# A linear-attention block with a routed MLP on one core: K's factor from one exponential, POOL's products moved, and the routing's work spread over six turns

## The chip, the core and the metric

The kernel runs on one core of a Trainium2 chip. Its time is the device time of one launch in microseconds; three runs of the kernel before took 224.96, 225.59 and 227.16 us, so the median is 225.59 us. A core has TensorE (PE, matrix products into PSUM), VectorE (DVE), ScalarE (ACT), GpSimd (POOL), and SyncE (SP), whose queue issues nearly all transfers here. Each engine takes its instructions in the order in which they were written, and waits at the first whose inputs or buffers are not ready.

## What is computed

Four batches of 768 tokens, 8 heads of 48 channels (C = 384). First a gated linear recurrence per head:

```python
for t in range(S):
    cur   = (u * k_t) outer v_t
    y_t   = r_t @ (state + cur)
    state = w_t[:, None] * state + k_t outer v_t
```

Then, on the heads laid side by side (x, 768 rows of 384 per batch), a routed MLP:

```python
scores  = x @ w_gate
top     = the 128 rows of the batch with the highest scores
out     = x
out[top] = x[top] + sigmoid(scores[top]) * (relu(x[top] @ w1) @ w2)   # w1 384x1024, w2 1024x384
```

## The kernel before

The recurrence is done in 24 chunks of 128 tokens (4 batches of 6), one chunk's output per turn of the loop at line 541; n numbers the turns, from -4 to 23. Decay products are taken in logs. For a chunk, `lnw` (L139, L143) takes lw = ln w and over = exp(-lw) on ACT. `sums` (L159) multiplies lw by a triangular matrix on PE, so that PSUM holds the log sums X; ACT then makes fall = exp(X) (L162), rise = exp(-X) (L165) and, from X's first row, the chunk's total decay in a line (L172), which a small transfer turns into a column, `all` (L176). `divided` (L183) makes kw = k * over on POOL, `scaled` (L216) K = kw * fall and R = r * rise on DVE. `turned` (L226, L228) transposes K and R on PE and copies them out on ACT. `scores` (L242), `fresh` (L258, the products of K and v, two halves per chunk), `masked` (L270, DVE), `states` (L285, L288 on DVE; L290 on POOL, mid * all), `from_state` (L301) and `from_chunk` (L318) make the chunk's output in the PSUM tile P, of which there are two. The token's own term goes beside: `own_products` (L192 r * k, L193 times u, both POOL), `own_sum` (L200, DVE), `own_values` (L207, POOL: vo = v * own). `result` (L332) adds P and vo into x on DVE, L338 takes the score, and L342 stores x.

The order is written out by hand. The loop body runs several chunks at once: turn n works on the state part of chunk n, the products of chunk n+1, the transposes of n+2, K and R of n+3 and the logs of n+4. The order within a turn is

```python
loads(n + 4); [one piece of w1 or w2, turns 2 to 8]
from_state(n); lnw(n + 4); divided(n + 3); scores(n + 1); fresh(n + 1); from_chunk(n)
mix(what[0]); turned(n + 2, "K"); turned(n + 2, "R"); masked(n + 1); states(n + 1); result(n)
sums(n + 4); scaled(n + 3); own_products(n + 3); own_values(n + 1); own_sum(n + 2); mix(what[1])
```

L192 carries an explicit wait (`sync`, L192): it starts only behind the same chunk's R on DVE. `loads(m)` (L107) issues on SP w of chunk m+4, k and r of m+3 and v of m+1, 192 KB each, from five or six buffers a name. SP's queue holds in a turn: four loads, a piece of a weight, the store of x, the `all` transfer. Ahead of the loop stand `loads(-4)` to `loads(-1)` and the broadcasts of u and w_gate (L508 to L513), 192 KB each too.

The routed part comes in two generators, taken in steps by `mix` from turn 6 on. `select(b)` (L349): copies every score to all partitions (L356 PE, L359 ACT), compares (L369, six DVE instructions), counts on PE (L379), ranks and picks on DVE (L384 to L393), turns the pick into indices (L400 PE, L404 DVE), gathers 128 rows with an indirect transfer on POOL's queue (L413), transposes them (L421, L423) and makes the gate (L428 to L444). `forward(b)` (L450): 8 steps of six products with w1 (L464), a relu on ACT every four steps (L469), 8 steps of products with w2 (L474), the gated sum on DVE (L480) and an indirect store (L483). A string such as "fssfsf" in `plan` (L493) says which steps, f or s, a turn takes. `forward(b)` begins in the fifth turn of the next batch. Behind the loop (L573) come a test of the value range, which all engines load (L581), the rest of `forward(2)`, `select(3)` and `forward(3)`.

PSUM's eight banks: four for the two P tiles, two shared by name "r" (transposes), one "m" (log sums, and select's products), one "f" (forward's products).

Of the kernel before, what the change touches and what calls it, by code (L numbers as in the profile page):

```python
# [35 lines left out]
def kernel(  # L36
# [30 lines left out]
    assert 0 < CAP < S and CAP % L != 1 and B * NCH < 256  # L67
# [26 lines left out]
    work = {n: {} for n in range(N)}  # L94

    def load(name, n):
        if not 0 <= n < N:
            return
        b, ci = chunks[n]
        x, bufs = dict(w=(w, 5), k=(k, 5), r=(r, 5), v=(v, 6))[name]  # L100
        t = lev.tile([L, H, D], FP32, tag=name, name=name, bufs=bufs)
        nc.sync.dma_start(  # L102
            out=t, in_=x[b, :, ci * L:(ci + 1) * L, :].rearrange("h t d -> t h d")
        )
        work[n][name] = t

    def loads(n):  # L107
        load("w", n + 4)
        load("k", n + 3)
        load("r", n + 3)  # L110
        load("v", n + 1)
# [23 lines left out]
    def lnw(n):  # L135
        if 0 <= n < N:
            t = work[n]
            t["lw"] = lev.tile([L, C], FP32, tag="lw", name="lw", bufs=2)
# [3 lines left out]
            t["over"] = lev.tile([L, C], FP32, tag="over", name="over", bufs=3)  # L142
            nc.scalar.activation(out=t["over"], in_=t["lw"], func=AF.Exp, scale=-1.0)  # L143
# [9 lines left out]
    def sums(n):  # L153
        if not 0 <= n < N:
            return
        t = work[n]
        lw = t.pop("lw")
        ps = psM.tile([L, 512], FP32, tag="m", name="ps_x")
        nc.tensor.matmul(ps[:, 0:C], tri, lw, start=True, stop=True)  # L159
        t["fall"] = lev.tile([L, C], FP32, tag="fall", name="fall")  # L160
        t["rise"] = lev.tile([L, C], FP32, tag="rise", name="rise")
        nc.scalar.activation(  # L162
            out=t["fall"], in_=ps[:, 0:C], func=AF.Exp, accum_out=guard[:, n, 1:2]
        )
# [4 lines left out]
        if chunks[n][1] > 0:  # L169
            line = line_bufs[n % len(line_bufs)]  # L170
            t["all"] = all_bufs[n % len(all_bufs)]
            nc.scalar.activation(  # L172
                out=line[:, :, 0:D, :].rearrange("o q d j -> o j q d"), func=AF.Exp,
                in_=ps[0:1, 0:C].rearrange("o (j q d) -> o j q d", q=2, d=D),
            )
            nc.sync.dma_start(out=t["all"], in_=line.rearrange("o q d j -> o (q d j)"))  # L176

    def divided(n):
        if not 0 <= n < N:
            return  # L180
        t = work[n]
        t["kw"] = lev.tile([L, H, D], FP32, tag="kw", name="kw")
        nc.gpsimd.tensor_mul(  # L183
            t["kw"], t["k"], t.pop("over").rearrange("p (h d) -> p h d", d=D)
        )

    def own_products(n):
# [4 lines left out]
        sync(nc.gpsimd.tensor_mul(rk, t.pop("r"), t.pop("k")), t["scaled"], "one port")  # L192
# [16 lines left out]
    def scaled(n):  # L209
# [5 lines left out]
        for to, of, by in (("K", "kw", "fall"), ("R", "r", "rise")):  # L215
            t["scaled"] = nc.vector.tensor_mul(  # L216
                t[to][:, :, 0:D], t[of], t.pop(by).rearrange("p (h d) -> p h d", d=D)
            )
# [126 lines left out]
    groups = [(c0, min(L, CAP - c0)) for c0 in range(0, CAP, L)]  # L345

    chosen = {}

    def select(b):  # L349

        every = mod.tile([L, S], FP32, name="every")
        for hf in range(2):
            ps = psM.tile([L, NHF, L], FP32, tag="m", name="ps_e")
# [9 lines left out]
            yield  # L363

        ahead = mod.tile([L, NCH, S], BF16, name="ahead")
        won = mod.tile([L, NCH], FP32, name="won", bufs=2)
        for c in range(NCH):
            lo = c * L
            nc.vector.scalar_tensor_tensor(  # L369
# [6 lines left out]
        ps = psM.tile([L, NCH], FP32, tag="m", name="ps_r")  # L376
        for c in range(NCH):
            for e in range(c + 1):
# [3 lines left out]
                )  # L382
        rank = mod.tile([L, NCH], FP32, name="rank", bufs=2)
        nc.vector.tensor_sub(rank, behind_n, won)  # L384
        nc.vector.tensor_add(rank, ps, rank)

        for gi, (c0, n) in enumerate(groups):
            pick = mod.tile([L, NCH, L], BF16, name="pick")
            at = rank
            if c0 > 0:  # L390
                at = mod.tile([L, NCH], FP32, name="at")
                nc.vector.tensor_scalar_add(out=at, in0=rank, scalar1=float(-c0))
            nc.vector.tensor_tensor(  # L393
                out=pick, in0=_heads(slots, NCH), in1=at.to_broadcast([L, NCH, L]),
                op=ALU.is_equal,
            )
            yield
            ps = psM.tile([L, 2], FP32, tag="m", name="ps_i")
            for c in range(NCH):
                nc.tensor.matmul(  # L400
                    ps, pick[:, c, :], ids[:, b, c, :], start=(c == 0), stop=(c == NCH - 1)
                )
            idx = mod.tile([L, 1], UINT32, name="idx", bufs=2)
            nc.vector.tensor_scalar(  # L404
                out=idx, in0=ps[:, 0:1], scalar1=ps[:, 1:2], scalar2=float(b * S),
                op0=ALU.add, op1=ALU.max,
            )
            rows = views[b][0:b + 1].rearrange("b s c -> (b s) c")
            where = bass.IndirectOffsetOnAxis(ap=idx[0:n, 0:1], axis=0)
            xe = mod.tile([L, C], FP32, name="xe", bufs=2)  # L410
            if n < L:
                nc.vector.memset(xe, 0.0)
            nc.gpsimd.indirect_dma_start(  # L413
                out=xe[0:n], out_offset=None, in_=rows, in_offset=where,
                bounds_check=(b + 1) * S - 1, oob_is_err=False,
            )
            yield

            ps = psM.tile([L, NDC, L], FP32, tag="m", name="ps_x")
            for dc in range(NDC):  # L420
                nc.tensor.transpose(ps[:, dc, :], xe[:, dc * L:(dc + 1) * L], ident)  # L421
            xeT = mod.tile([L, NDC, L], FP32, name="xeT", bufs=2)
            nc.scalar.copy(out=xeT, in_=ps)  # L423
            yield

            own = mod.tile([L, 1], FP32, name="own", bufs=2)
            scr = lev.tile([L, C], FP32, tag="scr", name="scr")
            nc.vector.tensor_tensor_reduce(  # L428
                out=scr, in0=xe, in1=wg_bc, scale=1.0, scalar=0.0, op0=ALU.mult, op1=ALU.add,
                accum_out=own,  # L430
            )
            neg = mod.tile([L, 1], FP32, name="neg", bufs=2)
            nc.vector.scalar_tensor_tensor(
                out=neg, in0=own, scalar=-1.0, in1=own, op0=ALU.mult, op1=ALU.min
            )
            nc.scalar.activation(out=neg, in_=neg, func=AF.Exp)
            den = mod.tile([L, 1], FP32, name="den", bufs=2)
            nc.vector.tensor_scalar_add(out=den, in0=neg, scalar1=1.0)
            nc.vector.reciprocal(out=den, in_=den)
            gate = mod.tile([L, 1], FP32, name="gate", bufs=2)  # L440
            nc.vector.scalar_tensor_tensor(
                out=gate, in0=own, scalar=0.0, in1=neg, op0=ALU.is_ge, op1=ALU.max
            )
            nc.vector.tensor_mul(gate, gate, den)  # L444
            chosen.setdefault(b, []).append((n, rows, where, xe, xeT, gate))
            yield
# [213 lines left out]
```

## Time and profile before

| | |
|---|---|
| median of three runs | 225.59 us |
| the profiled execution | 223.47 us, of it 221.6 us from the first to the last instruction |
| busy | PE 172.4, DVE 141.6, POOL 117.6, ACT 102.2 us |
| start of x (L332) in turns 0, 5, 11, 20, 23 | 27.87, 55.40, 100.35, 169.51, 188.67 us |
| transfers | 29.38 MB; four loads and one store of 192.0 KB a turn, 3 pieces of 512.0 KB and 4 of 384.0 KB |
| granted TensorE clock, mean | 0.931 |

How to read it: a page gives the busy time of each engine, the span in 40 slices, the chain of work that ended last, and the costliest groups of instructions with the idle time ahead of each and what ended it. The timeline gives every instruction's start and duration, so the starts of L332 mark the turns. Busy time is an average over stages; the prediction takes the stages one by one.

### The profile page before, as it was taken

To read this page: it belongs to the slowest core of one execution; us is meant where nothing else is said; L and a number is where in the kernel's file an instruction comes from. 1 tells how busy PE (TensorE), PEld (TensorE's weight loads), DVE (VectorE), ACT (ScalarE), POOL (GpSimd) and SP (SyncE) were. 2 spreads that over 40 slices of the span, in tenths; PEclk is the share of its full clock that TensorE was granted. 3 is DMA by queue.
4 is the path that set the end of the run, shared out by engine and by line. 5 is a ranking of instruction groups with operands and counts; after the bars stand their busy time and mean duration, and the time that the engine had idled before them with its cause. 6 is when DMAs were issued, how large, how long until landed. Compare 5 with 4: busy or idle time off the path is not lost.

```text
span 221.6 us, 8505 instructions
## 1 busy us (share of the span) xinstructions
PE 172.4 (78%) x3586; PEld 138.2 (62%) x3586; DVE 141.6 (64%) x329; ACT 102.2 (46%) x261; POOL 117.6 (53%) x137
## 2 busy tenths in 40 slices
PE   2697677797859766897799869978898598686990
PEld 0465466676648665796687657867876467553950
DVE  6443177777546998695769986976499834281301
ACT  4685645476852722755666426656642101110110
POOL 3750578887176669775546497745654931001101
PEclk9998899999985985999999969999999769999997
DMA  6998997878989996996899884622011022101101
GB/s 130 209 186 168 192 176 163 177 137 224 233 199 210 213 209 166 198 230 149 180 201 210 180 179 100 157 63 73 3 40 40 4 70 74 38 1 36 38 7 40
DMA packets 108542, 29.38 MB, mean 133 GB/s; under 512 B 103376, under 2 KB 107728, under 8 KB 108496
## 3 DMA queue, kind: packets, MB, share of 16 engines
q1 hardware_dynamic: 107984, 27.18, 56.5%
q0 software_dynamic: 512, 1.57, 2.1%
q8 instruction: 30, 0.49, 1.0%
q14 instruction: 16, 0.13, 0.2%
HBM read 23.20 MB, written 5.51 MB: 130 GB/s over the span
## 4 chain that ended last, share of the span: by engine, by line
PE 27%; DVE 21%; issue 13%; POOL 11%; DMA 9%; ACT 9%; SPq 8%; POOLq 0%; DVEq 0%; ACTq 0%
SPq L102 6%; DMA all_buf<-line_buf 5%; PE ps_p L318 5%; PE ps_f L464 5%; DVE ahead L369 5%; PE ps_t L226 5%; POOL rk L192 3%; DVE scr L338 3%; POOL vo L207 3%; DVE x L332 3%; PE ps_f L474 3%; POOL rk L193 2%; DVE k_buf L216 2%; DMA xe<-out_dram,idx 2%; PE ps_p L242 2%
## 5 line engine op out<-in xcount | busy, mean ns | idle before, releaser
L192 POOL TENSOR_TENSOR rk<-r,k 128x384 f32<-128x384 f32 x24 | 24.4, 1015 | 20.7 <-DVE r_buf L216 19.4
L228 ACT COPY Kt<-ps_t 128x512 f32<-128x512 f32 x24 | 14.0, 585 | 45.1 <-PE ps_t L226 45.1
L318 PE MATMUL ps_p<-v,sc 64*64 64x48 f32 x768 | 30.8, 230 | 4.4 <-issue 2.6
L290 POOL TENSOR_TENSOR s<-mid,all_buf 128x192 f32<-128x192 f32 x20 | 12.2, 610 | 38.7 <-DMA all_buf<-line_buf 24.1
L318 PEld LDWEIGHTS ps_p<-v,sc 64*64 64x64 f32 x768 | 28.0, 146 | 5.6 <-issue 3.0
L159 PE MATMUL ps_x<-lw,tri 128*128 128x384 f32 x48 | 23.9, 585 | 6.4 <-ACT lw L139 6.4
L369 DVE SCALAR_TENSOR_TENSOR ahead<-every,score,behind 128x768 bf16<-128x768 f32 (+5 forms) x24 | 23.4, 1024 | 8.2 <-ACT every L359 8.2
L464 PE MATMUL ps_f<-xeT,w 128*128 128x128 f32 x192 | 24.5, 278 | 4.5 <-ACT hid L469 3.9
L464 PEld LDWEIGHTS ps_f<-xeT,w 128*128 128x128 f32 x192 | 23.1, 192 | 7.5 <-ACT hid L469 4.5
L193 POOL TENSOR_TENSOR rk<-rk,u_bc 128x384 f32<-128x384 f32 x24 | 25.2, 1050 | 1.9
L183 POOL TENSOR_TENSOR kw<-k,over 128x384 f32<-128x384 f32 x24 | 24.4, 1018 | 3.0 <-DMA k<-in_k_dram 2.9
L474 PE MATMUL ps_f<-w,hid 128*128 128x384 f32 x64 | 25.3, 529 | 0.7 <-ACT hid L469 0.7
L270 DVE TENSOR_TENSOR sc<-ps_p,mask 128x512 f32<-128x512 f32 x24 | 16.4, 682 | 14.7 <-PE ps_p L258 14.7
L332 DVE TENSOR_TENSOR x<-ps_p,vo 128x384 f32<-128x384 f32 x24 | 13.3, 552 | 17.4 <-POOL vo L207 14.5
L207 POOL TENSOR_TENSOR vo<-v,own 128x384 f32<-128x384 f32 x24 | 23.2, 966 | 0.0
L242 PE MATMUL ps_p<-Rt,Kt 48*64 48x64 f32 x768 | 17.7, 229 | 5.6 <-DVE x L332 3.2
L301 PEld LDWEIGHTS ps_p<-s,Rt 48*64 48x64 f32 x704 | 13.5, 135 | 13.4 <-issue 7.3
L242 PEld LDWEIGHTS ps_p<-Rt,Kt 48*64 48x64 f32 x768 | 15.0, 141 | 7.3 <-ACT over L143 2.0
L226 PE MATMUL ps_t<-ident,k_buf 128*128 128x128 f32 x96 | 18.7, 327 | 0.0
L301 PE MATMUL ps_p<-s,Rt 48*64 48x48 f32 x704 | 16.4, 223 | 2.5 <-DVE mid L288 2.5
L474 PEld LDWEIGHTS ps_f<-w,hid 128*128 128x128 f32 x64 | 12.6, 208 | 8.0 <-issue 1.8
L226 PE MATMUL ps_t<-ident,r_buf 128*128 128x128 f32 x96 | 17.2, 310 | 0.0
(77 smaller groups left out, 301.8 us busy)
## 6 DMA issues: line engine op xcount, KB each, us to landing
w<-in_w_dram SPq DMA_DIRECT2D x24, 192.0 KB, 4.0
k<-in_k_dram SPq DMA_DIRECT2D x24, 192.0 KB, 4.4
r<-in_r_dram SPq DMA_DIRECT2D x24, 192.0 KB, 4.7
v<-in_v_dram SPq DMA_DIRECT2D x24, 192.0 KB, 4.0
out_dram<-x SPq DMA_DIRECT2D x24, 192.0 KB, 2.8
w<-in_moe_w_dram SPq DMA_DIRECT2D x3, 512.0 KB, 5.2
w<-in_moe_w_dram SPq DMA_DIRECT2D x4, 384.0 KB, 5.2
all_buf<-line_buf SPq DMA_DIRECT2D x20, 2.0 KB, 2.6
```

What stands on the lines that cost most here:

```text
L159: nc.tensor.matmul(ps[:, 0:C], tri, lw, start=True, stop=True)
L183: nc.gpsimd.tensor_mul(t["kw"], t["k"], t.pop("over").rearrange("p (h d) -> p h d", d=D))
L192: sync(nc.gpsimd.tensor_mul(rk, t.pop("r"), t.pop("k")), t["scaled"], "one port")
L193: nc.gpsimd.tensor_mul(rk, rk, u_bc)
L207: nc.gpsimd.tensor_mul(t["vo"], t["v"], t.pop("own").to_broadcast([L, H, D]))
L226: nc.tensor.transpose(ps[:, j, :], t[name][:, 2 * j:2 * j + 2, :], ident)
L242: nc.tensor.matmul(P[half(sub), par, j * HB:(j + 1) * HB], t["Kt"][half(par, D), j, half(sub)], t["Rt"][half(par, D), j, half(sub)], start ...
L301: nc.tensor.matmul(t["P"][half(sub), par, j * D:(j + 1) * D], t["Rt"][half(par, D), j, half(sub)], t["s1" if sub else "s0"][half(par, D), ...
L318: nc.tensor.matmul(t["P"][half(sub), par, j * D:(j + 1) * D], t["sc"][half(sub), par, j, :], t["v"][half(sub), 2 * j + par, :], start=(sub ...
L369: nc.vector.scalar_tensor_tensor(out=ahead[:, c, lo:S], in0=every[:, lo:S], scalar=score[:, b, c:c + 1], in1=behind[:, 0:S - lo], op0=ALU. ...
L464: nc.tensor.matmul(ps[:, q, :], w1[:, dc, (f0 + q) * L:(f0 + q + 1) * L], xeT[:, dc, :], start=(dc == 0), stop=(dc == NDC - 1),)
L474: nc.tensor.matmul(ps, hid[:, fc, :], w2[:, fc, :], start=(fc == 0), stop=(fc == NFC - 1))
```

## The change

- `over` and `kw` go. In their place `without` (DVE) takes X, read from PSUM, less the chunk's lw, and `falls` (ACT) makes fall = exp of that from SBUF; K = k * fall directly.
- `sums` keeps only the product and rise; fall and the total's line are made a turn later, the line by `totals`.
- POOL: L183 goes; vo is made at the head of the turn; r * k waits for the latest DVE instruction marked `latest["two"]`: R, or a comparison or pick that follows R in the turn. `own_sum` stays at the end of the turn, behind these.
- Loads: `loads(m)` comes at the end of a turn, behind the store of x, three chunks ahead instead of four, in the order v, k, r, w. `all` now stands in front of the store. k and r get six buffers, lw three. Ahead of the loop only `loads(-4)` to `loads(-2)` remain, and the first v (chunk 0) and v of chunk 1 are the 10th and the 14th of the 192 KB transfers on SP, where they were the 12th and the 17th.
- The routed part: `select` ends with the comparisons, `chosen_rows` (x) does ranks to transposes, `gates` (g) the gate. Their PSUM tiles move from bank "m" to the "r" pair and "f". A plan of six turns says what each does at three places; `forward(b)` begins six turns behind `select(b)` (turn 12 for batch 0) instead of four, so that `forward(2)` lies wholly behind the loop. There the order is written out in a string.

```diff
     def loads(n):
-        load("w", n + 4)
+        load("v", n + 1)
         load("k", n + 3)
         load("r", n + 3)
-        load("v", n + 1)
+        load("w", n + 4)
...
     def sums(n):
-        lw = t.pop("lw")
-        ps = psM.tile([L, 512], FP32, tag="m", name="ps_x")
-        nc.tensor.matmul(ps[:, 0:C], tri, lw, start=True, stop=True)
+        ps = t["X"] = psM.tile([L, 512], FP32, tag="m", name="ps_x")
+        nc.tensor.matmul(ps[:, 0:C], tri, t["lw"], start=True, stop=True)
...
+    def without(n):
+        t["less"] = lev.tile([L, C], FP32, tag="less", name="less")
+        nc.vector.tensor_sub(t["less"], t.pop("X")[:, 0:C], t.pop("lw"))
+
+    def falls(n):
+        t["fall"] = lev.tile([L, C], FP32, tag="fall", name="fall")
+        nc.scalar.activation(
+            out=t["fall"], in_=t.pop("less"), func=AF.Exp, accum_out=guard[:, n, 1:2]
+        )
...
-        sync(nc.gpsimd.tensor_mul(rk, t.pop("r"), t.pop("k")), t["scaled"], "one port")
+        sync(nc.gpsimd.tensor_mul(rk, t.pop("r"), t.pop("k")), latest["two"], "one port")
...
     plan = [
-        ("", "fsfsss"), ("", "fssfsf"), ("", "fsf"), ("s", "fff"), ("s", "sfff"), ("", "fff")
+        ("f", "sx", "ss"), ("", "ffff", "ss"), ("", "ff", "s"),
+        ("", "xff", "xx"), ("", "xffff", "xg"), ("g", "ffff", "g"),
     ]
...
+            from_state(n)
+            own_values(n + 1)
+            totals(n + 3)
+            without(n + 3)
+            lnw(n + 4)
+            scores(n + 1)
+            fresh(n + 1)
+            from_chunk(n)
+            turned(n + 2, "K")
+            turned(n + 2, "R")
+            falls(n + 3)
+            masked(n + 1)
+            states(n + 1)
+            result(n)
+            mix(what[0])
+            if n >= 2 * NCH and n % NCH == 0:
+                steps["f"] = forward(n // NCH - 2)
+            sums(n + 4)
+            mix(what[1])
+            scaled(n + 3)
+            mix(what[2])
+            own_products(n + 3)
+            own_sum(n + 2)
+            for m in range(max(n - 1, -4) if n <= AHEAD else n, n if n < AHEAD else n + 1):
+                loads(m + AHEAD)
...
+        mix("fsxffffsssssffffxxxffxx")
+        steps["g"] = gates(B - 2)
+        mix("gggffffff")
```

## The prediction

> **What bounds the kernel now.** I read the table of stages first, then the chain of waits inside one stage, then the timeline for the prices of single instructions. Stages, by the starts of x: up to turn 0, turns 0 to 5, 5 to 12, 12 to 18, 18 to 23, and what lies behind the loop.
>
> ```profile
> core 0: us, PE busy (x) PEld busy (x) DVE busy (x) ACT busy (x) POOL busy (x), PEclk, DMA share, GB/s
> 0.00:27.90 27.90, 17.63 (x242) 12.53 (x242) 11.58 (x34) 18.14 (x45) 12.16 (x25) 0.94 0.90 177
> 27.90:55.40 27.50, 21.48 (x642) 17.82 (x642) 20.18 (x45) 15.17 (x42) 21.50 (x25) 1.00 0.82 175
> 55.40:107.20 51.80, 40.57 (x985) 34.58 (x985) 38.46 (x85) 27.49 (x73) 34.00 (x36) 0.87 0.89 201
> 107.20:152.50 45.30, 39.24 (x899) 32.65 (x897) 36.64 (x78) 25.57 (x65) 28.90 (x31) 0.96 0.69 151
> 152.50:188.70 36.20, 30.73 (x679) 24.54 (x677) 25.76 (x62) 11.83 (x30) 17.87 (x19) 0.91 0.12 41
> 188.70:221.60 32.90, 22.71 (x148) 16.12 (x146) 8.99 (x30) 4.03 (x8) 3.13 (x3) 0.95 0.08 27
> ```
>
> No engine is full in any stage of the loop: in turns 0 to 5 POOL has 21.5 of 27.5 us, in 12 to 18 PE 39.2 of 45.3 and DVE 36.6. So order and waits cost time. The chain of waits shows the early ring, one turn long:
>
> ```profile
> 41.68 0.99 POOL rk L192
> 42.75 1.00 POOL rk L193
> 43.74 0.80 POOL vo L207
> 44.57 0.57 DVE x L332
> 45.16 0.75 DVE scr L338
> 45.92 0.77 DVE k_buf L216
> 46.69 0.48 DVE r_buf L216
> 47.24 1.00 POOL rk L192
> ```
>
> r * k waits for R, vo stands behind it on POOL, x waits for vo, R stands behind x on DVE: 5.56 us a turn with nothing else in it. Up to turn 12 transfers come on top (share 0.89 with the weights), and POOL's L290 waits 24.1 us in all for `all`, whose small transfer stands behind four loads on SP. The third loss is two engines at once on SBUF operands:
>
> ```profile
> 122.19 1.07 DVE L369 SCALAR_TENSOR_TENSOR ahead<-every,score,behind 128x128 bf16<-128x128 f32 x1
> ```
> ```profile
> 198.04 0.35 DVE L369 SCALAR_TENSOR_TENSOR ahead<-every,score,behind 128x128 bf16<-128x128 f32 x1
> ```
>
> The same comparison takes 1.07 us beside POOL's L207 and L183, and 0.35 us behind the loop, where POOL is idle.
>
> **The change, part by part.** Turn prices are from the timeline.
>
> *DVE.* From the start of `masked` at 99.10 to the end of `own` at 102.83 a turn's nine instructions take 3.73 us. `without` adds one (PSUM and SBUF in, 128x384): between the 0.35 us of L285 at half the width and the 0.85 us of L216 beside POOL; nearest is L332, same operands and shape, 0.55. I take 0.58 with its gap and 0.1 for what is left of contention on the score: 4.4 us a turn. The routed part, uncontended behind the loop: six comparisons from 194.67 to 198.43, 3.76; ranks 0.34; pick 0.96; index 0.22; gate 1.4; ye 0.62: 7.3 a batch. So 6 x 4.4 + 7.3 = 33.7 a batch, 5.6 us a turn. r * k now waits for R or a comparison, so these run before POOL's products, not beside them.
>
> The Trainium skill, "VectorE: DVE Perf Modes", section on the TRN2 errata, speaks against reading X from PSUM: its table gives DVE a fixed 120 cycles from PSUM against 58 from SBUF, about 0.06 us at 0.96 GHz. The rows show no such gap (0.552 for L332 from PSUM, 0.549 for K from SBUF); by the rule 24 instructions would add 1.5 us to DVE, by the rows nothing.
>
> *POOL.* L183 goes (24 x 1.02 us). Left are 0.83 + 0.51 + 2 x 1.0 and gaps, 3.5 us of a turn of 5 or more. vo of a chunk is made a turn before x needs it, so the ring above is cut. Behind the waiting r * k stand L193, the next vo and L290: from R they end after 3.5 us, and s0 is wanted only by the next turn's L285. The gather (1.05 us of POOL) stands before r * k, and delays it by that in one turn of six.
>
> *ACT.* exp(-lw) goes (24 x 0.52), fall reads SBUF (0.52 by L139, instead of 0.49). The line (0.84) reads another order: between the 0.48 of rise and 1.7, twice itself; I take 0.84. Sum 3.7 us a turn, hidden behind DVE and PE, and at 5 us and more a turn 1.7 would be too. But fall now stands behind the copies Kt and Rt: from the end of `turned` 0.86 to Rt's end, 0.68 to fall, then K. A turn's K needs it only after x and the score, so I cost it at nothing; cover gone, see the third rival.
>
> *PE.* One turn without routed work, from 117.96 to 121.92: 3.96 us. `forward` has 16 steps in 5.36 + 5.33 us (205.17 to 210.53, 210.63 to 215.96), `select`'s products 2.6 (1.1 + 0.66 + 0.3 + 0.55). So (6 x 3.96 + 10.7 + 2.6) / 6 = 6.2 us a turn from 12 on, 4.4 in turns 6 to 11. Today PE's queue stands still at the indices: L400 waits 2.42 us for the pick in one turn, and the transposes behind it run 1.09 us instead of 0.66. After the change the products stand a turn behind the pick.
>
> "TensorE: Matmul & The Clock Gate", Part 1, says that one idle window of about 3.4 us halves the clock. That speaks against turns 6 to 11, which lose their `forward` steps and leave PE 2 us a turn idle. By the rule such gaps cost nothing; by the row of 2.42 us a turn could cost 2.6 us more (3.96 x 0.66).
>
> *Transfers and SP.* A full stretch (8 to 13 us) moves 200 GB/s, so 0.197 MB takes 0.98 us and a turn's five 4.9. Loads now wait on SP behind the store, thus for x; they are needed three turns later, and five transfers with a landing of 4.7 take 10 of those 15 us. `all` passes in front of the store and of one turn's loads.
>
> *The sum*, as starts of x:
> - Turn 0, today 27.87. v of chunk 1 lands at 20.37 as the 17th transfer; as 14th it lands 3 x 0.98 earlier, at 17.4. Then `fresh` and `from_chunk` (0.6 + 1.7 in the slow rows there): 19.8. Bounds: 18, and 23 if the added step to K is late.
> - Turns 1 to 5, today 5.5: 5.0 by transfers (4.9) and DVE (4.4): 44.8.
> - To turn 11, today 7.5 a turn. v of chunk 12 has 58 loads and 9 stores at or before it, 13.2 MB, and 3.1 MB of weights: 16.3 / 0.2 = 81.4 us; with 0.8 for the start, 2.3 for landing and 1.3 for the two products, 86. DVE alone would allow 44.8 + 6 x 5.6 = 78.
> - Nine turns to 20, today 7.68: PE 6.2, with 0.4 for what the engines lose on each other: 6.6, 145.4. Bounds 6.2 and 7.68.
> - Turns 21 to 23 are short (no more logs, then no transposes, then no `scores`). From x to x PE has: transposes 1.05, two steps 1.3, state part to `from_chunk` 2.25, 4.6; the same with L379, 5.3; L400, four steps, L301 and L318, 3.1. With 0.5 for waits: 158.9, today 188.67.
> - Behind the loop 32.9 today. The last batch's counts (L379) wait for eight `forward` steps now: today they end 9.9 us behind x, then 10.5; with rank and pick 1 us later: 33.9. Bounds 32 and, in slow rows, 38.
>
> 158.9 + 33.9 = 192.8 of span, with the 1.87 around it 194.7 against 223.47. That execution was 0.9% below its median, so 194.7 x 225.59 / 223.47 = 196.5 us.
>
> **Rivals.**
> 1. *Later turns keep their pace.* If in turns 12 to 20 it is not the crossing of queues that costs but the round trips themselves, 7.68 stays: 9 x 1.08 = 9.7 more, 206. For it: PE had 87% in 107 to 152. Against: DVE's 36.6 us there hold some 5 us a batch of contention.
> 2. *Transfers bind.* If the rate is the 185 GB/s that I get as mean of the first 25 slices, 16.3 / 0.185 = 88.1 puts turn 11 at 92.5: 203. For it: a share of 0.82 even in the stage without weights. Against: 201 GB/s held over 52 us.
> 3. *The longer row to K takes the place of the ring* (slower). It decides at K on DVE: if K waits in every turn for `turned`, Rt's copy and fall (1.05 + 0.86 + 0.68) and DVE's turn and `forward`'s steps follow in line, a turn is 2.6 + 4.4 + 1.9 = 8.9 us: 19.8 + 23 x 8.9 + 33.9 + 1.9 = 260. From (188.67 - 19.8 - 1) / 23 = 7.3 us a turn it is no gain. Against it: the row runs while DVE does own, less, masked, the states and x of the next turn (3.3 us).
>
> **How the numbers follow.** Forecast 0.52; first rival 0.20; second 0.16; third 0.06; a pace just at 7.3, 0.03; better than 190, 0.03. So faster by over 1% 0.91, within 1% (about what a measurement tells from no change) 0.03, slower 0.06. The forecast's own range is 190 to 202. The full range is 187 (6.2 a turn, early start) to 212 (first rival with a slow tail).
>
> **What would show it.** Right: x of turn 0 near 20 and of turn 11 near 86; no wait of x for vo; the comparison of 128 columns at 0.35 to 0.5 us; turns near 6.6 from 12 on with PE at 90% or more; L290's wait for `all` under 8 us. Wrong: DVE's K waiting over 1 us a turn for fall; a clock of 0.6 in turns 6 to 11; PE idle at the log sums, because ACT or `without` frees the bank late; a tail over 36 us.

## The result, and the profile after

Four runs of the changed kernel took 203.46, 205.06, 205.91 and 207.33 us, median 205.49, against 225.31 for four runs of the kernel before. The ratio is 0.9075, 95% interval 0.8983 to 0.9168: faster by 9%, where 196.5 us was forecast, within a range of 187 to 212. The profiled execution took 205.91 us, with a span of 204.1.

| start of x in turn | 0 | 5 | 11 | 20 | 23 | end of span |
|---|---|---|---|---|---|---|
| before | 27.87 | 55.40 | 100.35 | 169.51 | 188.67 | 221.6 |
| forecast | 19.8 | 44.8 | 86 | 145.4 | 158.9 | 192.8 |
| after | 21.20 | 50.37 | 92.51 | 150.89 | 165.92 | 204.1 |

The table of stages of the changed kernel, cut at these starts:

```profile
core 0: us, PE busy (x) PEld busy (x) DVE busy (x) ACT busy (x) POOL busy (x), PEclk, DMA share, GB/s
0.00:21.20 21.20, 14.37 (x206) 9.77 (x207) 12.74 (x38) 10.39 (x28) 9.15 (x21) 1.00 0.84 161
21.20:50.40 29.20, 23.98 (x671) 19.11 (x670) 21.73 (x51) 14.72 (x45) 17.56 (x21) 0.89 0.90 190
50.40:92.50 42.10, 36.95 (x839) 30.26 (x838) 35.80 (x75) 20.75 (x59) 19.87 (x22) 0.75 0.90 207
92.50:150.90 58.40, 54.82 (x1324) 47.37 (x1325) 52.79 (x123) 29.08 (x88) 34.70 (x40) 0.97 0.78 167
150.90:165.90 15.00, 14.44 (x376) 12.40 (x375) 11.00 (x30) 3.79 (x11) 6.32 (x8) 1.00 0.17 56
165.90:204.10 38.20, 28.92 (x177) 21.74 (x176) 11.26 (x42) 4.51 (x10) 4.19 (x4) 0.91 0.09 29
```

The nine turns from 11 to 20 take 58.4 us, 6.49 a turn, with PE busy for 54.82 of them: there PE is now the fullest engine, at 94%, as forecast (DVE has 90%). From turn 0 to turn 11 that is not so: a DMA share of 0.90 stands beside a PE with a granted clock of 0.75 to 0.89. And the stretch behind the loop has grown from 32.9 to 38.2 us, with 28.92 us of PE in it against 22.71.

The ring that the prediction read in the kernel before is gone from the trace. One turn of the changed kernel, by the timeline (start, duration, engine, operation; in brackets the idle time just before and what ended it):

```profile
39.15 0.56 DVE L220 TENSOR_TENSOR k_buf<-k,fall 128x384 f32<-128x384 f32 x1 [0.78 <-ACT fall L187]
39.63 0.55 DVE L220 TENSOR_TENSOR r_buf<-r,rise 128x384 f32<-128x384 f32 x1
40.26 1.00 POOL L196 TENSOR_TENSOR rk<-r,k 128x384 f32<-128x384 f32 x1 [2.31 <-DVE r_buf L220]
41.33 1.00 POOL L197 TENSOR_TENSOR rk<-rk,u_bc 128x384 f32<-128x384 f32 x1
42.29 0.83 POOL L211 TENSOR_TENSOR vo<-v,own 128x384 f32<-128x384 f32 x1
42.65 0.56 DVE L336 TENSOR_TENSOR x<-ps_p,vo 128x384 f32<-128x384 f32 x1 [0.68 <-PE ps_p L322]
```

x starts while vo of the next chunk still runs, and what it waits for is PE. The contention of DVE with POOL was mostly moved, not removed. The comparison of 128 columns that had taken 1.07 us takes 0.34, but POOL's products then run beside the next turn's score and K:

```profile
76.04 0.34 DVE L373 SCALAR_TENSOR_TENSOR ahead<-every,score,behind 128x128 bf16<-128x128 f32 x1
79.24 1.00 POOL L196 TENSOR_TENSOR rk<-r,k 128x384 f32<-128x384 f32 x1
80.31 1.00 POOL L197 TENSOR_TENSOR rk<-rk,u_bc 128x384 f32<-128x384 f32 x1
80.56 1.17 DVE L342 CUSTOM_DVE_ANT_0 scr<-x,wg_bc 128x384 f32<-128x384 f32 x1
81.27 1.15 POOL L211 TENSOR_TENSOR vo<-v,own 128x384 f32<-128x384 f32 x1
81.66 1.17 DVE L220 TENSOR_TENSOR k_buf<-k,fall 128x384 f32<-128x384 f32 x1
```

Over the whole run the 24 comparisons fall from 1024 ns in the mean to 678, 8.3 us in all, while the mean of a score is 812 ns (675 before), of a K 756 (599 before) and of an R 588 (547 before), 8.0 us more in all. The list of waits shows what else was named (engine, operation and line, who ended the wait: us in all, times, longest):

```profile
ACT lw L140 <- DMA w<-in_w_dram: 33.2, 17, 3.8
DVE k_buf L220 <- ACT fall L187: 12.6, 13, 2.2
POOL s L294 <- DMA all_buf<-line_buf: 11.8, 4, 3.9
PEld ps_x L157 <- ACT lw L140: 11.1, 8, 4.2
```

K waits for fall 13 times, 12.6 us in all, half a us a turn over 24 turns, so the longer row to K did not take over. The largest new wait is for a transfer: ln waits 33.2 us for w, which is now the last of a turn's four loads.

### The profile page after: what moved, and what is told of

Its sections match the earlier page's. It is cut to its first block, busy times and chain, and to the rows that moved or that the text cites. A ratio compares the mean times of both kernels' runs of the same rounds, so it can differ in the third digit from the quotient of the medians.

```text
span 204.1 us, 8458 instructions
## 1 busy us (share of the span) xinstructions
PE 173.5 (85%) x3586; PEld 140.6 (69%) x3586; DVE 145.3 (71%) x353; ACT 83.2 (41%) x237; POOL 91.8 (45%) x113
## 4 chain that ended last, share of the span: by engine, by line
PE 44%; SPq 14%; DMA 13%; issue 12%; DVE 8%; POOL 3%; ACT 2%; POOLq 0%; ACTq 0%
SPq L103 12%; PE ps_f L471 8%; PE ps_f L481 8%; PE ps_p L322 7%; PE ps_t L230 6%; PE ps_p L305 4%; PE ps_x L157 4%; PE ps_p L246 3%; DMA v<-in_v_dram 3%; PE ps_p L262 2%; DMA r<-in_r_dram 2%; DMA w<-in_w_dram 2%; DMA out_dram<-x 2%; DVE k_buf L220 2%; DMA all_buf<-line_buf 2%
## 5 line engine op out<-in xcount | busy, mean ns | idle before, releaser
L157 PE MATMUL ps_x<-lw,tri 128*128 128x384 f32 x48 | 26.1, 632 | 11.6 <-ACT lw L140 8.2
L220 DVE TENSOR_TENSOR k_buf<-k,fall 128x384 f32<-128x384 f32 x24 | 18.1, 756 | 12.6 <-ACT fall L187 12.6
L294 POOL TENSOR_TENSOR s<-mid,all_buf 128x192 f32<-128x192 f32 x20 | 12.3, 615 | 31.5 <-DMA all_buf<-line_buf 11.8
L140 ACT ACTIVATE lw<-w 128x384 f32<-128x384 f32 x24 | 12.5, 520 | 33.2 <-DMA w<-in_w_dram 33.2
L232 ACT COPY Kt<-ps_t 128x512 f32<-128x512 f32 x24 | 13.9, 579 | 21.8 <-PE ps_t L230 21.8
L305 PEld LDWEIGHTS ps_p<-s,Rt 48*64 48x64 f32 x704 | 15.0, 149 | 11.0 <-issue 5.6
L481 PE MATMUL ps_f<-w,hid 128*128 128x384 f32 x64 | 22.2, 493 | 0.2 <-ACT hid L476 0.2
L246 PE MATMUL ps_p<-Rt,Kt 48*64 48x64 f32 x768 | 19.2, 237 | 1.2 <-issue 1.2
L342 DVE CUSTOM_DVE_ANT_0 scr<-x,wg_bc 128x384 f32<-128x384 f32 x24 | 19.5, 812 | 0.8
L157 PEld LDWEIGHTS ps_x<-lw,tri 128*128 128x128 f32 x48 | 8.7, 227 | 14.9 <-ACT lw L140 11.1
L305 PE MATMUL ps_p<-s,Rt 48*64 48x48 f32 x704 | 18.0, 237 | 0.9 <-DVE mid L292 0.9
L246 PEld LDWEIGHTS ps_p<-Rt,Kt 48*64 48x64 f32 x768 | 16.3, 149 | 2.6 <-issue 1.5
L274 DVE TENSOR_TENSOR sc<-ps_p,mask 128x512 f32<-128x512 f32 x24 | 16.3, 681 | 1.5 <-PE ps_p L262 1.5
```

The costliest lines, as they stand in the source:

```text
L157: nc.tensor.matmul(ps[:, 0:C], tri, t["lw"], start=True, stop=True)
L220: latest["two"] = nc.vector.tensor_mul(t[to][:, :, 0:D], t[of], t.pop(by).rearrange("p (h d) -> p h d", d=D))
L246: nc.tensor.matmul(P[half(sub), par, j * HB:(j + 1) * HB], t["Kt"][half(par, D), j, half(sub)], t["Rt"][half(par, D), j, half(sub)], start ...
L305: nc.tensor.matmul(t["P"][half(sub), par, j * D:(j + 1) * D], t["Rt"][half(par, D), j, half(sub)], t["s1" if sub else "s0"][half(par, D), ...
L481: nc.tensor.matmul(ps, hid[:, fc, :], w2[:, fc, :], start=(fc == 0), stop=(fc == NFC - 1))
```

## The experiments

There are twelve, in three groups of four, each group on a chip of its own. The kernel before had medians of 223.3, 223.6 and 224.0 us there. The last run is the changed kernel itself, 204.05 us, on the third chip; on the first two it was not run again. So 204.05 to 205.49 is what "no change" means below, and differences of 1 or 2 us in the median are not resolved.

### vo back in the ring

```diff
             from_state(n)
-            own_values(n + 1)
...
             own_products(n + 3)
+            own_values(n + 1)
             own_sum(n + 2)
```

> The changed kernel with vo made at its old place, behind r * k and its product with u on POOL, instead of at the head of the turn. Theory (the ring through POOL was what held the early turns, and cutting it is what the change gained there): the ring is back without kw, R to r * k 1.07, times u 1.0, vo 0.83, x 0.58, score 0.7, K 0.7, R 0.48, so 5.4 us plus the comparisons that r * k now also waits for (about 1.0 a turn on average): DVE waits for vo again, turns 6 to 20 go from 6.7 to about 7, the time to 209 to 214 us. Rival (the gain came from the transfers and from kw's removal, and vo's place costs nothing): 205 to 207 us, no wait of x for vo.

Four runs, 201.37 to 206.44 us, median 204.58: no loss. The ring is there again, as the waits of this run say:

```profile
DVE x L336 <- POOL vo L211: 20.2, 20, 2.3
```

Twenty waits, a us each, and no time lost: x of turn 5 stands at 50.41, where it stood at 50.37. So in this kernel cutting the ring did not pay. A wait with a large sum is a cost only if nothing else would have ended later.

### The loads as before

```diff
-        load("v", n + 1)
+        load("w", n + 4)
         load("k", n + 3)
         load("r", n + 3)
-        load("w", n + 4)
+        load("v", n + 1)
...
+        loads(-1)
...
         for n in range(-4, N):
+            loads(n + 4)
...
-            for m in range(max(n - 1, -4) if n <= AHEAD else n, n if n < AHEAD else n + 1):
-                loads(m + AHEAD)
```

> The changed kernel with the loads as before: at the head of the turn, four chunks ahead, in the order w, k, r, v, and loads(-1) ahead of the loop. Theory (the new order is worth the early start alone): x of turn 0 moves from 21.2 back to about 26, but ln w no longer waits for w (33.2 us in all now), so turns 1 to 5 fall from 5.83 to about 5.2 and most of the loss is made up by turn 11: 205 to 210 us. Rival (the transfers are where the gain came from): the time goes most of the way back, 216 us or more, with POOL waiting for the total's transfer over 20 us.

210.82 us (209.43 to 214.27; ratio to before 0.953, interval 0.917 to 0.989): 5 to 7 us lost by the medians, just above the theory and well below the rival. x of turn 0 goes back from 21.20 to 28.74, of turn 11 only from 92.51 to 97.88, and in turn 23 3.5 us are left of it (169.37 against 165.92). So the gain of the loads is the early start, and part of it melts on the way. POOL's wait for `all` goes from 11.8 to 28.3 us, without a loss of its own in turns 12 to 20 (50.8 us for the eight turns from 12 to 20, where the changed kernel has 51.7).

### w first

```diff
+        load("w", n + 4)
         load("v", n + 1)
         load("k", n + 3)
         load("r", n + 3)
-        load("w", n + 4)
```

> The changed kernel with w first instead of last among the four loads (w, v, k, r), nothing else. Theory (turns 1 to 5 missed my 5.0 us because ln w of chunk n+4 waits for the transfer that was issued last): ACT's wait for w falls from 33 to under 10 us, turns 1 to 5 from 5.83 to 5.2 or less, the time to 201 to 204 us. Rival (the rate of the transfers binds, and one name's wait only turns into another's): the wait moves to v or k, and the time stays within 1.5 us of 205.5.

206.25 us (203.53 to 206.49): no gain, so the theory falls and the rival holds. ln's wait for w falls from 33.2 to 4.5 us, PE's loads for `fresh` wait for v instead (8.4 us, 1.5 with w last), and x of turn 5 is at 50.13, of turn 11 at 90.72. The order of the four loads decided here who waits, not how long.

### The weights later

```diff
-            if 0 <= n - 2 < len(weights):
-                to, of = weights[n - 2]
+            if 0 <= n - 8 < len(weights):
+                to, of = weights[n - 8]
```

> The changed kernel with the seven pieces of w1 and w2 issued in turns 8 to 14 instead of 2 to 8, nothing else. Theory (transfers set the end of turn 11: 16.3 MB had moved by then at 180 to 190 GB/s): 1.5 MB less stands in front of turn 11, x of turn 11 starts at 85 to 87 us instead of 92.5, turns 2 to 7 at 5.5 to 6.5 us, and the time is 199 to 202 us. Rival (something else holds turns 1 to 11, the order of the engines or the slow TensorE clock): x of turn 11 at 90 or later and 204 to 207 us.

198.65 us (196.97 to 203.96; ratio 0.8942, interval 0.8755 to 0.9129). The table of stages of this run:

```profile
core 0: us, PE busy (x) PEld busy (x) DVE busy (x) ACT busy (x) POOL busy (x), PEclk, DMA share, GB/s
22.10:48.20 26.10, 21.22 (x677) 17.71 (x676) 21.65 (x51) 14.47 (x44) 15.93 (x20) 1.00 0.93 193
48.20:83.40 35.20, 29.80 (x838) 24.89 (x836) 32.43 (x77) 20.10 (x59) 20.40 (x24) 0.95 0.90 192
83.40:143.90 60.50, 55.26 (x1327) 47.38 (x1328) 53.77 (x122) 30.16 (x88) 35.95 (x39) 0.97 0.86 197
```

x of turn 11 starts at 83.39 us, 9.1 earlier and below the theory's 85 to 87, with the same instructions on every engine; the rate is no higher (193 and 192 GB/s), there is only less to move: 15.5 MB by then, where it was 17.7. So transfers did bind the stretch to turn 11. The granted clock rose there too, from 0.75 to 0.95, but it does not explain the gain: with 0.92 in the same turns the loads as before took 40.0 us and the second run with the old factor (below) 41.6, against 35.2 here. Turns 11 to 20 take 60.5 us, where the weights now pass; the runs with the same order there and the weights early took 58.4 to 60.9. Turns 1 to 5 take 5.2 us each, not the 5.0 of the forecast: the DMA share is 0.93 even with no weights in them.

### vo back in the ring, with the weights later

> The changed kernel with vo back behind r * k on POOL (the ring R to r * k to vo to x to R) and with the weights' pieces in turns 8 to 14, so that transfers no longer hide what the ring costs. Theory (the ring of some 5.5 us was a bound only hidden by transfers in the run with vo late alone): turns 1 to 7 at 5.5 us or more instead of 5.2 to 5.3 (x of turn 5 at 49.5 to 51, where the run with late weights alone has 48.2), 2 to 4 us longer than that run, 200 to 203. Rival (the ring is no bound in any stage): within 1.5 us of 198.65.

200.73 us (199.49 to 202.0). That is 2.1 above the run with late weights alone, whose times span 197 to 204; but on the same chip the run with late weights and a new tail (further down; its tail is worth half a us) took 197.15 to 199.34, so that all four times here lie above all six there. The ring costs some 2 us here, the low end of the theory, but not in turns 1 to 5. x of turn 5 starts at 48.31, with late weights alone at 48.16. One turn of the ring there:

```profile
37.51 0.56 DVE L336 TENSOR_TENSOR x<-ps_p,vo 128x384 f32<-128x384 f32 x1 [0.80 <-POOL vo L211]
38.61 0.56 DVE L220 TENSOR_TENSOR k_buf<-k,fall 128x384 f32<-128x384 f32 x1
39.09 0.55 DVE L220 TENSOR_TENSOR r_buf<-r,rise 128x384 f32<-128x384 f32 x1
39.72 1.00 POOL L196 TENSOR_TENSOR rk<-r,k 128x384 f32<-128x384 f32 x1 [1.78 <-DVE r_buf L220]
40.79 1.00 POOL L197 TENSOR_TENSOR rk<-rk,u_bc 128x384 f32<-128x384 f32 x1
41.74 0.84 POOL L211 TENSOR_TENSOR vo<-v,own 128x384 f32<-128x384 f32 x1
42.62 0.56 DVE L336 TENSOR_TENSOR x<-ps_p,vo 128x384 f32<-128x384 f32 x1 [1.19 <-POOL vo L211]
```

From x to x the ring is 5.11 us here, against 5.56 in the kernel before: its score and K are not beside POOL (0.56 each, where they were 0.75 and 0.77). It is as long as what the transfers allow, so in turns 1 to 5 it costs nothing. From x of turn 5 to x of turn 11 this run needs 40.3 us against 35.2, and there x waits for vo in all six turns, 7.9 us in all; with late weights alone it does so in no turn. In the first of the six, 2.6 us longer, POOL's L294 waits 4.3 us for `all`, with r * k, vo and so x behind it. In the last three, 3.4 us longer together, r * k stands behind the comparisons, the pick and the gather, so that these lie in the ring too. The turn with the pick:

```profile
75.58 0.56 DVE L336 TENSOR_TENSOR x<-ps_p,vo 128x384 f32<-128x384 f32 x1 [0.80 <-POOL vo L211]
77.13 0.55 DVE L220 TENSOR_TENSOR r_buf<-r,rise 128x384 f32<-128x384 f32 x1
78.06 0.96 DVE L397 TENSOR_TENSOR pick<-slots,rank 128x768 bf16<-128x768 f32 x1
79.09 0.99 POOL L196 TENSOR_TENSOR rk<-r,k 128x384 f32<-128x384 f32 x1 [2.97 <-DVE pick L397]
81.12 0.83 POOL L211 TENSOR_TENSOR vo<-v,own 128x384 f32<-128x384 f32 x1
81.99 0.56 DVE L336 TENSOR_TENSOR x<-ps_p,vo 128x384 f32<-128x384 f32 x1 [1.18 <-POOL vo L211]
```

From x to x it takes 6.41 us, with late weights alone 5.56. So in turns 6 to 11 the ring is a bound that the transfers hid.

### r * k no longer behind the comparisons

```diff
-            latest["two"] = nc.vector.scalar_tensor_tensor(
+            nc.vector.scalar_tensor_tensor(
...
-        latest["two"] = nc.vector.tensor_tensor(
+        nc.vector.tensor_tensor(
             out=pick, in0=_heads(slots, NCH), in1=rank.to_broadcast([L, NCH, L]),
```

> The changed kernel with one thing taken back: r * k waits on POOL only for the same chunk's R, not for the comparisons and the pick that follow R on DVE. Theory (DVE is near its limit in turns 6 to 20, so what the order saves there is time): the comparisons run beside POOL's two products again, 128 columns at about 1.07 us instead of 0.35, some 4 us a batch more on DVE; 3 batches in the loop, so 210 to 214 us against 205.5, and the turns 12 to 20 at 7.0 us instead of 6.5. Rival (the order only moves the contention to the score and to K, or PE is the bound there): within 1.5 us of 205.5, turns 12 to 20 at 6.4 to 6.6.

203.76 us (201.45 to 204.92), ratio 0.9107, interval 0.8934 to 0.928: no loss, so the rival holds. The comparison of 128 columns in a later batch is back beside POOL:

```profile
113.43 1.09 DVE L373 SCALAR_TENSOR_TENSOR ahead<-every,score,behind 128x128 bf16<-128x128 f32 x1
```

while the mean score falls from 812 to 743 ns. The time is the rival's, but turns 12 to 20 take 6.78 us each, between the 6.4 to 6.6 of the rival and the 7.0 of the theory; with w first they take 6.75, so this is within what these runs differ by. The contention of DVE and POOL is paid in one place or in another.

### The old factor, twice

First in the places of the changed kernel, where fall = exp(X) stands behind the transposes' copies on ACT:

```diff
+            t["over"] = lev.tile([L, C], FP32, tag="over", name="over", bufs=3)
+            nc.scalar.activation(out=t["over"], in_=t["lw"], func=AF.Exp, scale=-1.0)
...
-        nc.vector.tensor_sub(t["less"], t.pop("X")[:, 0:C], t.pop("lw"))
+        nc.gpsimd.tensor_mul(
+            t["kw"], t["k"], t.pop("over").rearrange("p (h d) -> p h d", d=D)
+        )
...
-            out=t["fall"], in_=t.pop("less"), func=AF.Exp, accum_out=guard[:, n, 1:2]
+            out=t["fall"], in_=t.pop("X")[:, 0:C], func=AF.Exp, accum_out=guard[:, n, 1:2]
...
-        for to, of, by in (("K", "k", "fall"), ("R", "r", "rise")):
+        for to, of, by in (("K", "kw", "fall"), ("R", "r", "rise")):
```

> The changed kernel with K's factor made in the old way, at the new places: over = exp(-lw) on ACT, kw = k * over on POOL where the subtraction stood on DVE, fall = exp(X) from PSUM, K = kw * fall. So DVE has 0.55 us a turn less, POOL 1.0 us and ACT 0.52 us more. Theory (the new factor is a small part of the gain: POOL has room, 4.6 of 6 us and more): 206 to 209 us, most of the loss in turns 0 to 5 where a turn is shortest. Rival (the new factor carries the gain of the turns 12 to 20, since kw collides with DVE on SBUF and holds vo and s0): 213 us or more.

220.97 us (218.22 to 223.72), ratio 0.9825: nearly all the gain gone, as the rival's number said. But the waits name another reason than the rival's. Line numbers are four higher here:

```profile
PEld ps_x L159 <- ACT fall L191: 36.2, 23, 3.9
ACT Kt L236 <- PE ps_t L234: 30.7, 23, 3.0
...
DVE k_buf L224 <- POOL kw L182: 10.5, 9, 2.6
```

PE's next log sums wait in 23 turns for fall. X lies in the one bank "m", and here it is read out by an exp that stands on ACT behind the copies of Kt and Rt, which themselves wait for PE. In the changed kernel the subtraction on DVE reads X at the head of the turn. So the same old factor again, with fall moved up:

```diff
             totals(n + 3)
+            falls(n + 3)
...
-            falls(n + 3)
             masked(n + 1)
```

> As the run with the old factor, but with fall = exp(X) taken at the head of the turn, in front of the next ln on ACT, instead of behind the transposes of K and R; over on ACT and kw on POOL are there as in that run. Theory (that run's 15 us were lost because PE's next log sums wait for fall to free the one PSUM bank, 36.2 us of waits, not because of the extra work): 205 to 210 us, and PE's wait for fall at the log sums gone or under 5 us. Rival (the extra 1.0 us of POOL and 0.5 of ACT a turn cost it, and the bank is only what shows): 215 us or more.

206.29 us (204.33 to 208.68), ratio 0.9235, interval 0.9119 to 0.9351: 15 us came from moving one ACT instruction. POOL is busy for 117.7 us again, and the leading wait of this run is

```profile
DVE k_buf L224 <- POOL kw L182: 25.0, 18, 3.1
```

while the log sums wait for fall in no turn. So the new factor itself, POOL's product and ACT's exp that it saves, is worth 0 to 2 us, which is not clear of the noise. What counts is that X is read out early, ahead of the transposes' copies: in this run by fall on ACT, in the changed kernel by the subtraction on DVE.

### The routed steps in their old places

```diff
-        ("f", "sx", "ss"), ("", "ffff", "ss"), ("", "ff", "s"),
-        ("", "xff", "xx"), ("", "xffff", "xg"), ("g", "ffff", "g"),
+        ("", "fsfss"), ("", "fssfsf"), ("", "fxxxf"), ("xx", "ffff"), ("x", "gggfff"), ("", "fff")
     ]
-    rank_at, gate_at = 3, 4
+    rank_at, gate_at = 2, 4
...
-        mix("fsxffffsssssffffxxxffxx")
+        mix("sssfsfsfsfxxxfxxffff")
```

forward(b) begins in the fifth turn again, and the two places of a turn are ahead of the transposes and at its end.

> The changed kernel with the routed part's steps where they stood before the change: the old lumps (two stretches a turn, the first before the transposes of K and R), ranks and pick two turns behind the comparisons' start, gate in the fifth turn and forward(b) in the fifth turn of the same batch, and the old string behind the loop. New factor, new POOL order and new loads stay; the tiles stay in the new banks. Theory (turns 12 to 23 gained about 15 us because PE's products stand a turn behind what they wait for and forward is spread evenly): turns 12 to 20 back at 7.2 to 7.7 us, 212 to 218 us in all, with PE waiting for the pick again. Rival (it was the factor and the POOL order that paid there): 207 us or less, turns at 6.7 or less.

212.76 us (211.09 to 213.72), ratio 0.9591, interval 0.947 to 0.9712: 7 to 9 us, the lower end of the theory. The table of stages from turn 11 on, and PE's wait for the pick:

```profile
93.40:157.90 64.50, 58.14 (x1362) 48.46 (x1361) 55.86 (x126) 32.28 (x93) 36.21 (x37) 1.00 0.67 144
157.90:176.70 18.80, 14.86 (x347) 11.74 (x348) 11.61 (x31) 2.23 (x7) 7.44 (x8) 0.91 0.17 55
176.70:209.30 32.60, 22.78 (x148) 16.27 (x147) 9.02 (x30) 3.83 (x8) 3.13 (x3) 0.99 0.09 27
```
```profile
PEld L404 <- DVE pick L397: 4.8, 3, 2.5
```

Turns 11 to 20 take 7.17 us each instead of 6.49, turns 20 to 23 18.8 instead of 15.0, and the tail 32.6 instead of 38.2, as before the change. So the new places gain 6.1 + 3.8 and give back 5.6. With 0.9 up to turn 11 that is the 5.2 us between the two profiled executions; the medians say 7 to 9. PE's wait for the pick was 8.2 us in the kernel before and is absent in the changed one.

### The tail

Two of forward(2)'s steps go behind the last counts, and the last batch's transposes go to the r pair of banks.

```diff
-        ps = psM.tile([L, NDC, L], FP32, tag="f", name="ps_x")
+        pool, tag = (psR, "r") if b == B - 1 else (psM, "f")
+        ps = pool.tile([L, NDC, L], FP32, tag=tag, name="ps_x")
...
-        mix("fsxffffsssssffffxxxffxx")
+        mix("fsxffffsssssffxxxffxx")
...
-        mix("gggffffff")
+        mix("gggffff")
```

> The changed kernel with two edits behind the loop: the counts, ranks and pick of the last batch stand after six of forward(2)'s steps instead of after eight, and the last gathered rows are transposed through a bank of the pair r instead of f, so that they don't wait for forward(2)'s gated sum. Theory (my tail missed by 4.3 us because the last gather starts 1.8 us later and its transposes wait another 1.8 for the bank): the tail goes from 38.2 to about 34.5, the time to 201 to 203 us. Rival (PE has no more room there, or the slow clock decides): tail 37 to 39, time unchanged within 1.5 us.

204.04 us (203.28 to 204.86): the stretch behind the loop takes 36.1 us, not 34.5. And most of the 2.1 are not the edit's: with the old tail the same stretch took either about 38.2 us, with 28.9 of PE (the changed kernel, the old loads, w first), or 36.6, with 27.3 (r * k no longer behind the comparisons, late weights). The difference is whether the last 48 products with w1 run at a lowered clock (0.76 in the changed kernel), 7.25 us, or not, 5.6. Half a us is left. Together with the late weights:

> The changed kernel with the two edits that gained by themselves: the weights' pieces in turns 8 to 14, and behind the loop the last batch's counts two forward steps earlier with its transposes in the r pair of banks. If the two add (theory): 6 to 7 us below the control for the weights and 1 to 2 for the tail, 195.5 to 198 us, the stretch behind the loop at 34.5 to 36 us. Rival (the tail's 2 us in its own run were only TensorE's clock, since runs with no edit there had 36.5 to 36.7 too): the same as with the weights alone, 198 to 200.

198.1 us (six runs, 197.15 to 199.34; ratio 0.8876, interval 0.8818 to 0.8933), tail 36.1. That is 0.5 from the run with late weights alone, so the rival holds. It is the best version here. Its interval lies clear of that of the unedited changed kernel beside it:

> The changed kernel itself, unedited, on the chip of the three runs above, as what they are compared with. If the granted clock of 0.75 in its turns 6 to 11 belongs to the order of its work (theory), it shows again, below 0.85. If it belongs to that one execution (rival), it is 0.85 to 1.0 and the time is 1 to 3 us shorter than 205.5.

204.05 us (six runs, 201.0 to 208.5; ratio 0.9055, interval 0.897 to 0.9139). The clock in its turns 6 to 11 was 0.82, as the theory said, in an execution of 207.54 us. In the runs with w first and with the new tail, whose order is nearly the same there, it was 0.87, so its depth differs by execution. Nor does it belong to the new order: the kernel before has 0.85 in the same turns. It hardly costs: with 0.75 the stretch from x of turn 5 to x of turn 11 took 42.1 us, with 0.82 42.7, with 0.87 40.6 and 41.1.

## Why the prediction was right, and where it was not

The direction, the mechanism of turns 12 to 20 and the full range held; the forecast's own range of 190 to 202 did not. The time came out 9 us above the forecast. Of the 11.3 us of span put on (204.1 against 192.8), 4.2 are in turns 1 to 5 and 4.3 behind the loop, 1.4 up to turn 0 and 1.5 in turns 21 to 23; turns 6 to 11 add 0.9 and the nine turns to 20 give 1.0 back. One credit, for cutting the ring, did not show in the time. Of the signs that it named, a tail over 36 us, one of being wrong, came, and the wait of mid * `all` on POOL was 11.8 us and not under 8.

- *Turn 0*, forecast 19.8: 21.20. Right; undoing the loads brings back 28.74.
- *"Turns 1 to 5, today 5.5: 5.0 by transfers (4.9) and DVE (4.4): 44.8."* This term failed first: 29.2 us for five turns, 4.2 more than forecast. It took 200 GB/s for granted and left out that pieces of the weights pass there from turn 2 on. By the rates and lengths in the table of stages, the first 50.4 us moved 21.2 x 161 + 29.2 x 190 = 8.96 MB, a rate of 178. Three runs with no weights in these turns took 26.1 to 26.7 us for the five, so most of the 4.2 us are the weights' pieces.
- *"To turn 11 ... 16.3 / 0.2 = 81.4 us; ... 86."* Right mechanism, wrong size: 92.51. By turn 11 17.7 MB had passed at 191 GB/s (92.5 us of the table), more than the 16.3 that were counted, since loads run ahead of that v. So the second rival's mechanism set this stretch. That its 92.5 was met to a tenth is luck: more bytes went by at a higher rate, 191 instead of its 185 GB/s. Of the 6.5 us, 5.6 had been lost by turn 5. That transfers bind is shown by the run with late weights (83.39).
- *Nine turns at 6.6*: 6.49, and 6.5 to 6.8 in the other runs with this order and early weights. The forecast named the reason, products a turn behind the pick and an even spread, and the run with the old places shows 7.17 without it. That leaves half a us of the 7.68 of the kernel before for the rest of the change.
- *Turns 21 to 23*, forecast 13.5 us from x of turn 20 to x of turn 23: 15.0, as 4.9, 5.0 and 5.1. The third turn was put at 3.1, which is a wrong sum: L400 0.3 and four steps 2.7 (a quarter of 10.7) are 3.0 already, and L301 and L318 took 0.7 and 1.1 in the kernel before, so 4.8.
- *"Behind the loop 32.9 today ... 33.9."* This failed by 4.3 us. The prediction followed only the counts, which ended 11.5 us behind x (forecast 10.5). It did not count that four more forward steps (24 products, 2.94 us in one stretch) and forward(2)'s gated sum also come before the last transposes. The timeline of the changed kernel:

```profile
179.85 1.09 POOL L418 DMA_INDIRECT xe<-out_dram,idx  x1 [9.41 <-DVE idx L409]
184.28 0.62 DVE L486 SCALAR_TENSOR_TENSOR ye<-ps_f,gate,xe 128x384 f32<-128x384 f32 x1 [0.68 <-DVE wide L598]
184.95 0.55 PE L425 MATMUL ps_x<-ident,xe 128*128 128x128 f32 x3 [1.54 <-DVE ye L486]
```

  The gather starts 13.9 us behind x (12.1 before), the transposes 19.0 (15.4 before), since they need the bank that forward(2)'s gated sum empties. That is 3.6 us; 1.6 more are the 48 products with w1 behind them, 7.25 us instead of 5.6. In the run with the new tail the gather started 12.3 us behind x and the bank was another, and yet the transposes came only at 18.7, because forward(2)'s last steps and the loaded test still stand ahead of the transposes in PE's order.
- *The ring.* The prediction opened with it and credited its cut. Put back into the changed kernel, it costs nothing: in turns 1 to 5 it is 5.1 us, no longer than the transfers, and in turns 6 to 11 the transfers hide it. With the weights late it costs 5 us in turns 6 to 11 and some 2 us of the whole. So the ring is a real bound, but the transfers stood right behind it. The 5.56 that the trace of before showed held 0.4 us of contention.
- *K for fall, contention.* K waits half a us a turn for fall, where the prediction had put nothing; that is under the 1 us that it named as a sign of being wrong, and the cover mostly held. The comparisons are free of contention, as forecast, but nearly all of the time went to the score, K and R; the prediction had kept 0.1 us a turn for that, and a score alone became 0.14 longer, a K 0.16.

Two rules of the Trainium skill were weighed. "VectorE: DVE Perf Modes", section on the TRN2 errata, has a longer fixed time for PSUM operands; `without`, which reads X from PSUM, took 549 ns in the mean, and an undisturbed K from SBUF 0.56 us: the row was right. "TensorE: Matmul & The Clock Gate", Part 1, names an idle window of some 3.4 us as what lowers the clock. In turns 6 to 11 less did. Two windows, in the columns of the table of stages, and the product behind the gap:

```profile
60.85:64.26 3.41, 1.78 (x31) 1.40 (x27) 3.41 (x7) 1.60 (x3) 0.43 (x1) 1.00 1.02 266
64.26:71.09 6.83, 6.10 (x132) 4.96 (x133) 6.76 (x17) 2.25 (x7) 3.56 (x4) 0.50 0.83 191
```
```profile
64.99 1.62 PE L157 MATMUL ps_x<-lw,tri 128*128 128x384 f32 x2 [2.05 <-DVE less L180]
```

The granted clock falls to half at 64.26, 1.3 us into a gap of 2.05, after 3.4 us of which PE was busy for 1.78. The two log sums then take 1.62 us; the kernel before shows 0.81 for the pair. The measurement decides, and the forecast was right to keep that risk; by the stretches above its price was 1 to 2 us at most.

*What stays open.* By single edits the 20 us are: loads 5 to 7, places of the routed steps 7 to 9 (with the transposes behind the first of them again), factor 0 to 2, vo and the order behind the comparisons nothing as the kernel stands. If these add, 2 to 8 us are left. Not undone were select's products leaving bank "m", the reading of X a turn later, and the extra buffers. The two runs with the old factor show that 15 us can hang on when bank "m" is emptied, so it is a likely place, but this was not tried.

## What to carry to other kernels

A wait in the trace, even a whole ring of waits, is worth cutting only as far as the next bound lies below it: before crediting it, work out that next bound, here megabytes by the rate that the start of the kernel really reaches. When that bound is moved, look at the ring again: here it then cost some 2 us. When an operation is moved, ask which PSUM bank or buffer it empties and who on PE stands behind that; one exp behind a copy cost 15 us. And when work is moved out of a loop to its tail, count it into every chain of the tail, not only into the one that it stands next to.

## What the runs showed of the hardware

The exp that writes a chunk's total on one partition took 843 ns in the mean when it read PSUM in order and wrote SBUF with a stride, and 473 when it read PSUM with the stride and wrote in order, with 384 elements both times (the kernel before and the changed one):

```profile
L172 ACT ACTIVATE line_buf<-ps_x 1x384 f32<-1x384 f32 x20 | 16.9, 843 | 0.0
L169 ACT ACTIVATE line_buf<-ps_x 1x384 f32<-1x384 f32 x20 | 9.5, 473 | 0.0
```

And the rate of the transfers differed by stretch, at nearly the same share. In turns 1 to 5 of the three runs with late weights, where the loads of 192-byte rows and the stores of x pass nearly alone, it was 185 to 193 GB/s at a share of 0.90 to 0.93. In turns 6 to 11 with the weights' longer rows among them it was 207 to 219 at 0.89 to 0.95. Up to turn 0 it was 160 to 184 in the changed kernel and its variants.
